# Seven block products in place of eight for four fifths of the q and k projection, on one core of a Trainium2

## The chip, the cores and the metric

The kernel runs on one core of one Trainium2 chip. The metric is the device time of the whole program in microseconds (us): the median of three runs before the change is 1844.57 us (1844.24 to 1844.73). The engines are named as in the profile: PE (matrix products), DVE (vector), ACT (scalar, activation), POOL (GpSimd) and SP, whose queue issues the transfers. SBUF is the memory on the chip, PSUM the eight banks into which PE writes.

## The reference

The computation takes x (2048 tokens of 640 numbers) through attention with 32 heads of 20 and through a Fourier mixing of tokens and columns, and blends the two by a gate.

```python
qkv = (x @ wqkv).reshape(B, S, 3, H, Dh).transpose(2, 0, 3, 1, 4)
q, k, v = qkv[0], qkv[1], qkv[2]
p = softmax(einsum("bhqd,bhkd->bhqk", q, k) * Dh ** -0.5)
a = (p @ v).transpose(0, 2, 1, 3).reshape(B, S, D) @ wo
ya, yb = x @ dft_hid_re.T, x @ dft_hid_im.T
b = dft_seq_re @ ya - dft_seq_im @ yb
g = sigmoid((x * gate_w).sum(-1, keepdims=True))
out = g * a + (1 - g) * b
```

The change touches the first line only, and of it the columns of q and k: 640 columns of weights each, that is five blocks of 128 (ND = 5), for four blocks of 512 tokens.

## The kernel before, in words

Every float32 value is split into two parts of a shorter type (float32r): a copy rounded to the short type, and the remainder, rounded as well. `split` (L112) does it with a copy on one engine (L114 on ACT, L116 elsewhere) and a subtraction on another (L117). A product of two such values is three matmuls, `three` (L119 to L122): high by high, high by low, low by high.

Tokens lie transposed in `xs[t]`, t = 0 to 3, each with its two parts, five blocks of 128 input columns (`d`) and 512 tokens. The q and k projection yields one tile per output block c (0 to 4 for q, 5 to 9 for k) and token block t: `qk_tiles` (L337) sums five terms of three matmuls, 15 matmuls of 512 columns, in one PSUM bank; ACT copies the bank into a tile `p` (L345), POOL splits that (L116, L117), and SP stores it to `qk_scr` in DRAM. From there SP loads, for each pair of heads, the twelve pieces of a "stack" into `kst` and `qst`, on which the score matmuls run (`s_mm`, L188). A score matmul (L198) fills a bank, and a maximum over it (L200, DVE) frees it.

PSUM banks for q, k, v and scores come from one ring, `bank()` (L129): a new tile takes the bank of the tile five places earlier, and the matmul waits until that one has been read. One of the six places is set aside for attention's output (`av`, L249). The two others hold the hidden-transform sums `yp`.

The work in order of program: block 0 of q and k for four token blocks, with the first v products between them (`v_pair`, L357: two tiles of 15 matmuls of 320 columns; POOL clears the tile, ACT copies); the rest of v; then the other eight column blocks, in the order 1, 6, 2, 7, 3, 8, 4, 9, each with four token blocks. At the head of each of these stands a `segment` (L402): eight score matmuls (ten in one of them) and one tile of the hidden transform (`hid_tile`, L374: 30 matmuls of 320 columns on half the rows each, whose two sums ACT copies at L395 and POOL adds at L396). Four times two more steps of scores are put in (`run_s`, L417; a step is two score matmuls). By the end of that stage 41 steps (LEAD) and 8 hidden tiles (HEAD) are done; the main loop follows, in which attention, the rest of the hidden transform and the token transform are interleaved. Each engine runs its instructions in the order in which the program lists them; SP issues all transfers in one row and waits in place where a tile isn't ready.

The tiles rotate in pools of a fixed number of buffers: `p` 7, `raw` 5 (raw weights, 1024 columns), `part` 2 (split weights), `v` 2. The four stack tiles kst and qst are not in use until the first stack is loaded.

## Time and profile before

| | |
|---|---|
| median of 3 runs | 1844.57 us (1844.24 to 1844.73) |
| profiled execution | 1844.95 us, of which the span is 1843.2 us |
| mean granted PE clock | 1.000 |
| PE matmuls | 17568 |
| DMA, mean | 282.12 MB, 153 GB/s |
| first q and k, v, other q and k, main loop, tail | 0 to 21, to 106, to 249.5, to 1838, to 1843.2 us |

The table's stage ends are read from the timeline. In the profile's rows an instruction has its engine, its line, the tiles (out<-in) and the shape; a matmul row's duration overlaps with the next, so the distance of two starts is what a matmul costs. "[idle before <-releaser]" at the end tells how long the engine stood before that row and what let it go on.

### The profile page before, as it was taken

How to read it: one execution, taken by the hardware profiler on the slowest of the kernel's cores; microseconds unless marked ns; L12 is line 12 of the kernel's file. 1: busy time of each engine (PE TensorE's matmuls, PEld its weight loads, DVE VectorE, ACT ScalarE, POOL GpSimd, SP SyncE). 2: the span in 40 equal slices, each digit the busy share in tenths (PEclk: the TensorE clock that was granted, in tenths of full speed). 3: DMA queues.
4: the chain of work that ended last, by engine and by line, in shares of the span. 5: the costliest groups of instructions: out<-in, count | busy, mean ns of one | idle time of the engine just before them, and what ended most of it. 6: DMA issues, size and time to landing. Idle time of an engine off the chain costs nothing.

```text
span 1843.2 us, 44645 instructions
## 1 busy us (share of the span) xinstructions
PE 1835.5 (100%) x17568; PEld 1359.3 (74%) x17568; DVE 1382.1 (75%) x2344; ACT 1354.7 (73%) x2646; POOL 1000.1 (54%) x819
## 2 busy tenths in 40 slices
PE   9999999999999999999999999999999999999998
PEld 8988777676767777777777777777777777776666
DVE  4044458888887888888888888888888888888843
ACT  4222258788787888888888888888888877778885
POOL 5234532121136676344677788655668867745644
PEclk9999999999999999999999999999999999999999
DMA  7654341222135574547577676746485866532233
GB/s 235 165 148 158 137 127 56 80 65 69 56 93 172 179 218 147 150 126 196 176 206 227 181 241 201 193 140 183 148 230 182 248 190 188 172 92 63 75 100 109
DMA packets 181898, 282.12 MB, mean 153 GB/s; under 512 B 47843, under 2 KB 116067, under 8 KB 181687
## 3 DMA queue, kind: packets, MB, share of 16 engines
q1 hardware_dynamic: 181687, 279.26, 50.8%
q8 instruction: 138, 2.26, 0.5%
q14 instruction: 73, 0.60, 0.1%
HBM read 215.14 MB, written 64.05 MB: 151 GB/s over the span
## 4 chain that ended last, share of the span: by engine, by line
PE 97%; POOL 1%; issue 1%; ACT 0%; DMA 0%; SPq 0%; DVE 0%; POOLq 0%; ACTq 0%; DVEq 0%
PE ps L566 25%; PE yp L645 20%; PE ps L959 17%; PE ps L198 14%; PE yp L385 7%; PE ps L120 3%; PE ps L122 3%; PE ps L121 3%; PE yp L752 3%; POOL p L117 1%; DMA raw<-in_xa 0%; ACT p L345 0%; POOL p L116 0%; POOL raw L396 0%; PE ps L1045 0%
## 5 line engine op out<-in xcount | busy, mean ns | idle before, releaser
L200 DVE TENSOR_REDUCE mx<-ps 128x1 f32<-128x512 f32 x2048 | 1279.1, 683 | 311.5 <-PE ps L198 250.9
L961 ACT ACTIVATE p<-ps 128x512 f32<-128x512 f32 x2048 | 1053.6, 613 | 277.8 <-PE ps L198 154.9
L959 PE MATMUL ps<-qst,kst 62*128 62x512 f32 x1920 | 726.2, 406 | 0.1
L198 PE MATMUL ps<-kst,qst 60*128 60x512 f32 x1920 | 665.7, 410 | 0.0
L645 PE MATMUL yp<-x,part 64*128 64x320 f32 x5376 | 628.7, 306 | 0.0
L645 PEld LDWEIGHTS yp<-x,part 64*128 64x128 f32 x5376 | 602.4, 185 | 5.6
L566 PE MATMUL ps<-p,v 128*21 128x512 f32 (+1 forms) x4096 | 479.2, 595 | 0.0
L117 POOL TENSOR_TENSOR part<-raw,part 128x1024 fp32r<-128x1024 f32 (+1 forms) x128 | 287.5, 2246 | 335.3 <-ACT part L114 305.5
L959 PEld LDWEIGHTS ps<-qst,kst 62*128 62x128 f32 x1920 | 341.3, 185 | 162.8 <-DVE mx L200 97.4
L198 PEld LDWEIGHTS ps<-kst,qst 60*128 60x128 f32 x1920 | 322.3, 184 | 12.7 <-issue 4.2
L566 PEld LDWEIGHTS ps<-p,v 128*21 128x21 f32 (+1 forms) x4096 | 104.0, 101 | 244.5 <-issue 237.3
L385 PE MATMUL yp<-wb,x 64*128 64x320 f32 x1920 | 224.1, 307 | 0.0
L385 PEld LDWEIGHTS yp<-wb,x 64*128 64x128 f32 x1920 | 210.1, 186 | 6.0
L396 POOL TENSOR_TENSOR raw<-raw 128x320 f32<-128x320 f32 x64 | 55.5, 868 | 264.6 <-ACT raw L395 219.9
L525 POOL TENSOR_TENSOR raw<-raw,raw 128x1024 f32<-128x1024 f32 x77 | 187.6, 2437 | 0.0
L114 ACT ACTIVATE part<-raw 128x1024 fp32r<-128x1024 f32 (+2 forms) x123 | 123.7, 1006 | 0.9 <-DMA raw<-in_wfirst 0.9
L752 PE MATMUL yp<-x,part 64*128 64x320 f32 x768 | 102.2, 308 | 0.0
L345 ACT ACTIVATE p<-ps 128x512 f32<-128x512 f32 x40 | 23.8, 597 | 106.4 <-PE ps L122 76.4
L117 POOL TENSOR_TENSOR x<-araw,x 128x320 fp32r<-128x320 f32 x112 | 97.6, 879 | 1.3
L752 PEld LDWEIGHTS yp<-x,part 64*128 64x128 f32 x768 | 91.9, 186 | 1.1
L120 PE MATMUL ps<-x,part 128*128 128x512 f32 x200 | 80.0, 400 | 0.5
L121 PE MATMUL ps<-x,part 128*128 128x512 f32 x200 | 78.5, 392 | 0.8 <-DVE x L117 0.8
(98 smaller groups left out, 1346.0 us busy)
## 6 DMA issues: line engine op xcount, KB each, us to landing
raw<-in_cdft SPq DMA_DIRECT2D x192, 512.0 KB
araw<-a_scr SPq DMA_DIRECT2D x192, 160.0 KB
qk_scr<-p SPq DMA_DIRECT2D x40, 512.0 KB
kst<-qk_scr SPq DMA_DIRECT2D x90, 160.0 KB
qst<-qk_scr SPq DMA_DIRECT2D x90, 160.0 KB
yt<-y_scr SPq DMA_DIRECT2D x80, 160.0 KB
a_scr<-raw SPq DMA_DIRECT2D x64, 160.0 KB
y_scr<-yt SPq DMA_DIRECT2D x64, 160.0 KB
```

Source lines behind the costliest of these rows:

```text
L117: e2.tensor_tensor(dst2, src, f32(dst1), op=ALU.subtract)
L120: pe.matmul(ps, st1, mv1, start=first, stop=False)
L121: pe.matmul(ps, st1, mv2, start=False, stop=False)
L198: pe.matmul(ps, q[b : b + KROWS, qt * P : (qt + 1) * P], k[b : b + KROWS, kc * 512 : (kc + 1) * 512], start=True, stop=True)
L200: return lambda: dve.tensor_reduce(mx[n][:, h, qt, kc : kc + 1], ps, axis=AX.X, op=ALU.max)
L385: pe.matmul(yp[h][:, :HE], x[r, xz, d, cs], w[r, wz, d, :HE], start=d == 0 and z == 0, stop=d == ND - 1 and z == 2)
L525: pool.tensor_tensor(raws[0], raws[0], raws[1], op=ALU.add if PRODUCTS[n][0][1][0] > 0 else ALU.subtract)
L566: pe.matmul(t[32 * j : 32 * j + m, :], v[:, r : r + m], pp[qc][:, h, :], start=kt == 0, stop=kt == NS - 1)
L645: pe.matmul(yp[h][:, :HE], c[r, cz, cs], a[r, az], start=s == 0 and z == 0, stop=s == NS - 1 and z == 2)
L752: pe.matmul(yp[h][:, :HE], o[oz][r], wos[d, hf][r, wz], start=d == 0 and z == 0, stop=end)
L959: pe.matmul(pt, k[b : b + KROWS + 2, kt * P : (kt + 1) * P], q[b : b + KROWS + 2, qc * 512 : (qc + 1) * 512], start=True, stop=True)
L961: act.activation(pts[n, kt, qc][:, h], pt, AF.Exp, scale=float(DH) ** -0.5)
```

## The change

Blocks 1 to 4 of q and of k are taken in pairs (c, 5 + c), and the tokens in two halves, g = 0 (token blocks 0 and 1) and g = 1 (2 and 3). The four results of a pair and a half (q and k, two token blocks) are one 2 by 2 block product whose inner dimension is also cut in two: input blocks 0, 1 against 2, 3. It is computed by Winograd's form with seven products in place of eight; the products of input block 4 are added into p5, p2 and p4 as they are, and into p3 on a difference of token blocks. `quad` has the seven in the order p6, p7, p1, p5, p2, p4, p3, with 6, 6, 6, 9, 9, 9 and 9 matmuls, and after them the sums of products: ACT copies three banks, DVE makes six additions with a PSUM operand (L444), POOL one (L459). Each of the four results is then split by ACT (copy, L112) and POOL (subtraction, L115) and stored as before.

The form needs sums of tokens and of weights. `load_sums` loads the tokens of a half again in float32, makes five sums on POOL (L384) and splits them on ACT and DVE; they live where the stacks will be (kst, qst, and x3 in the first half; kst1, qst1 and the place of x0 in the second). x0 is loaded once more in the main loop (`reload_x`, on POOL). `load_pair` loads a pair's weights, makes five sums on POOL (`sums`, L403 to L407), splits the summed ones (`ready`: ACT and DVE, 256, 384 and 384 columns) and the rest (`parts`: 640 and 384 columns, subtractions on DVE in the first half and on POOL in the second). While quad c runs, the pair c + 1 is made ready: sums after p5, `ready` after p2, `parts` after p4.

The program's order becomes: block 0 for token blocks 0 and 1; 8 v pairs with the first half's sums; four quads of the first half, without segments; block 0 for token block 2, two v pairs, for token block 3, six v pairs, the last three with two steps of scores each; four quads of the second half, each with one segment before p6 and one after p5, the first also with two steps of scores after p2. Hidden tiles take token blocks 4 to 15 of 128 first. `raw` has 4 buffers, `part` 3, and the bank ring has six places until the main loop.

```diff
-    for t in kst:
-        pool.memset(f32(t), 1.0)
...
-        return work.tile([P, 1024], F32, name="raw", bufs=5)
+        return work.tile([P, 1024], F32, name="raw", bufs=4)
 
     def part_tile():
-        return work.tile([P, 2, 1024], R, name="part", bufs=2)
+        return work.tile([P, 2, 1024], R, name="part", bufs=3)
...
+    def load_sums(g):
+        a = {}
+        for i, k in ((1, 0), (1, 1), (0, 0), (0, 1)):
+            a[i, k] = pair_tile()
+            sp.dma_start(a[i, k], xa[2 * g + i, :, 2 * k : 2 * k + 2])
+        b = pair_tile()
+        sp.dma_start(b, xa[2 * g : 2 * g + 2, :, ND - 1].rearrange("t p c -> p t c"))
+        if g:
+            more = new_x(0).rearrange("p z d c -> p (z d c)")
+            homes = [kst[1], qst[1], more[:, :S], more[:, S : 2 * S], more[:, 2 * S : 2 * S + 1024]]
+        else:
+            homes = [*kst, *qst, xs[3].rearrange("p z d c -> p (z d c)")[:, :1024]]
+        ops[g] = [t.rearrange("p (z d c) -> p z d c", z=2, c=512) for t in homes]
+        yield
+        s1, s2, s3, s4, s5 = ops[g]
+        sums = (
+            (s1, a[1, 1], a[1, 0], a[1, 1], ALU.add),
+            (s3, a[1, 0], a[0, 0], a[1, 0], ALU.subtract),
+            (s2, a[0, 0], a[1, 1], a[0, 0], ALU.subtract),
+            (s4, a[0, 1], a[0, 1], a[0, 0], ALU.subtract),
+            (s5, b[:, :1], b[:, :1], b[:, 1:], ALU.subtract),
+        )
+        for t, u, u1, u2, op in sums:
+            pool.tensor_tensor(u, u1, u2, op=op)
+            yield
+            split(t[:, 0], t[:, 1], u, act, dve)
+            yield
+
+    ops = {}
+    T_AT = ((0, 1), (3, 4), (5, 6), (2, 7))
+    B_AT = ((0, 1), (2, 3), (5, 6), (4,), (7,))
+
+    def load_pair(c, e2=dve):
+        a, b = raw_tile(), raw_tile()
+        n = ND * P
+        for k, raw in ((c, a), (ND + c, b)):
+            sp.dma_start(raw[:, :n].rearrange("p (d c) -> p d c", d=ND), wqk[k])
+        near, far, t13 = [slice(2 * P * k, 2 * P * (k + 1)) for k in range(2)] + [slice(n, n + 2 * P)]
+        made = {}
+
+        def sums():
+            t1, t3, t2 = a[:, t13], b[:, t13], b[:, near]
+            pool.tensor_tensor(t1, b[:, near], a[:, near], op=ALU.subtract)
+            pool.tensor_tensor(t3, b[:, far], b[:, near], op=ALU.subtract)
+            pool.tensor_tensor(t2, b[:, far], t1, op=ALU.subtract)
+            for k, raw in enumerate((a, b)):
+                pool.tensor_tensor(raw[:, 7 * P :], a[:, (2 + k) * P : (3 + k) * P], t2[:, k * P : (k + 1) * P], op=ALU.subtract)
+
+        def ready():
+            t = made["t"] = part_tile()
+            for o, u in ((3 * P, b[:, near]), (5 * P, b[:, n:]), (0, a[:, n:])):
+                w = slice(o, o + u.shape[1])
+                split(t[:, 0, w], t[:, 1, w], u, act, dve)
+
+        def parts():
+            t = made["b"] = part_tile()
+            split(t[:, 0, :n], t[:, 1, :n], a[:, :n], act, e2)
+            split(t[:, 0, n:], t[:, 1, n:], b[:, 2 * P : n], act, e2)
+
+        return made, sums, ready, parts
+
+    def quad(c, g, w, between):
+        x, y = xs[2 * g], xs[2 * g + 1]
+        s1, s2, s3, s4, s5 = ops[g]
+        made = w[0]
+
+        def group(*terms):
+            ps = bank()
+            todo = []
+            for name, k, z in terms:
+                at = (T_AT if name == "t" else B_AT)[k]
+                todo += [(made[name][:, :, o * P : (o + 1) * P], z[:, :, d]) for d, o in enumerate(at)]
+            for k, (wo_, z) in enumerate(todo):
+                three(ps, wo_[:, 0], wo_[:, 1], z[:, 0], z[:, 1], k == 0, k == len(todo) - 1)
+            return ps
+
+        def done(st, i, j):
+            split(st[:, 0].bitcast(R), st[:, 1].bitcast(R), st[:, 1], pool if g and c == ND - 1 else act, pool)
+            r = (j * ND + c) * P
+            stores.append((qk_scr[:, 2 * g + i, r : r + P].rearrange("z p c -> p z c"), st))
+            flush(2)
+
+        def add(out_, a, b):
+            dve.tensor_tensor(out_, a, b, op=ALU.add)
+
+        o12, o22 = pair_tile(), pair_tile()
+        p6 = group(("t", 1, s2))
+        act.activation(o12[:, 1], p6, AF.Copy)
+        between(0)
+        p7 = group(("t", 2, s3))
+        o11, o21 = pair_tile(), pair_tile()
+        p1 = group(("b", 0, x[:, :, 0:2]))
+        act.activation(o11[:, 0], p1, AF.Copy)
+        add(o12[:, 1], o12[:, 1], p1)
+        add(o21[:, 1], o12[:, 1], p7)
+        p5 = group(("t", 0, s1), ("b", 4, y[:, :, ND - 1 :]))
+        act.activation(o22[:, 0], p5, AF.Copy)
+        add(o12[:, 1], o12[:, 1], p5)
+        pool.tensor_tensor(o22[:, 1], o21[:, 1], o22[:, 0], op=ALU.add)
+        between(1)
+        done(o22, 1, 1)
+        p2 = group(("b", 1, x[:, :, 2:4]), ("b", 3, x[:, :, ND - 1 :]))
+        add(o11[:, 1], o11[:, 0], p2)
+        done(o11, 0, 0)
+        between(2)
+        p4 = group(("t", 3, y[:, :, 2:4]), ("b", 3, y[:, :, ND - 1 :]))
+        add(o21[:, 1], o21[:, 1], p4)
+        between(3)
+        done(o21, 1, 0)
+        p3 = group(("b", 2, s4), ("b", 4, s5))
+        add(o12[:, 1], o12[:, 1], p3)
+        done(o12, 0, 1)
...
     def hid_tile(i, read_out):
+        if j == 0:
+            st = (st + 4) % NS
...
+    def quads(g, soon, rest):
+        for c in range(1, ND):
+            this = soon[c - 1]
+            after = soon[c] if c + 1 < ND else None
+
+            def between(k):
+                if k == 0:
+                    if c + 2 < ND:
+                        soon.append(load_pair(c + 2, pool if g else dve))
+                    elif c + 2 == ND:
+                        soon.extend(rest[0]())
+                elif k == 1 and g:
+                    lead(0, 5, 8, 2)
+                if k and after:
+                    after[k]()
+                elif k in (1, 2):
+                    rest[k]()
+                if g and k == 2 and c == 1:
+                    run_s(step + 2)
+                if g and k == 2 and c == ND - 1:
+                    load_v(0)
+
+            if g:
+                lead(0, 5, 6, 4, 0) if c == ND - 1 else lead(0, 5, 8, 2)
+            quad(c, g, this, between)
+
+    fins = []
+    quads(0, soon, (lambda: fins.extend(load_wqk(k) for k in (0, ND)) or [], lambda: fins.pop(0)(), lambda: fins.pop(0)()))
+    fin = load_x(3)
+    pool.memset(f32(kst[0]), 1.0)
+    qk_tiles((0, ND), 2)
+    v_pair(0, 8)
+    fin()
+    sums = load_sums(1)
+    next(sums)
+    v_pair(0, 10)
+    qk_tiles((0, ND), 3)
+    flush()
+    stack = list(load_stack(0))
+    for s in (12, 14):
+        v_pair(0, s)
+        flush()
+        for args in stack[3 * s - 36 : 3 * s - 30]:
+            sp.dma_start(*args)
+        next(sums)
+        if s == 14:
+            next(sums)
+    soon = [load_pair(1, pool)]
+    for s in range(8, NS, 2):
+        v_pair(1, s)
+        if s == 8:
+            flush()
+            fin = load_wb(2)
+        else:
+            run_s(step + 2)
+        if s < 14:
+            next(sums), next(sums)
+        if s == 10:
+            fin()
+        if s == 12:
+            soon[0][1]()
+            soon[0][2]()
+            soon.append(load_pair(2, pool))
+        if s == 14:
+            next(sums)
+            soon[0][3]()
+    make_gate()
+    quads(1, soon, (lambda: fins.append(load_wb(3, act, pool)) or [], lambda: fins.pop()(), lambda: None))
+    pool.memset(f32(kst[1]), 1.0)
+    xs[0] = new_x(0)
+    av["name"] = places.popleft()
+    av["tile"] = place_tile(av["name"])
...
+    for k, d in enumerate(range(0, ND, 2)):
+        prepare(1 + 4 * k, 4 + 4 * k, reload_x, d)
```

In the second half DVE stands for c = 1, from p2's addition to the start of the next segment, as follows (ps0 to ps5 are banks; L444 frees the bank that it reads, L198 in this numbering is the maximum over scores, L115 the remainder of `split`):

```order
L444 TENSOR_TENSOR p_1648<-p_1648,ps5_1742 128x512
L115 TENSOR_TENSOR part_1756<-raw_1502,part_1756 128x256
L115 TENSOR_TENSOR part_1756<-raw_1502,part_1756 128x384
L115 TENSOR_TENSOR part_1756<-raw_1501,part_1756 128x384
L198 TENSOR_REDUCE mx_1414<-ps0_1763 128x1
L198 TENSOR_REDUCE mx_1414<-ps1_1765 128x1
L198 TENSOR_REDUCE mx_1414<-ps2_1769 128x1
L198 TENSOR_REDUCE mx_1414<-ps3_1771 128x1
L444 TENSOR_TENSOR p_1649<-p_1649,ps4_1775 128x512
L444 TENSOR_TENSOR p_1627<-p_1627,ps5_1794 128x512
L198 TENSOR_REDUCE mx_1414<-ps0_1808 128x1
L198 TENSOR_REDUCE mx_1414<-ps1_1810 128x1
```

In the stage of before, DVE has these rows from the end of one segment to the head of the next (L200 is the maximum there, L117 the remainder):

```order
L200 TENSOR_REDUCE mx_1024<-ps3_1238 128x1
L200 TENSOR_REDUCE mx_1024<-ps4_1240 128x1
L117 TENSOR_TENSOR part_1274<-raw_1111,part_1274 128x640
L200 TENSOR_REDUCE mx_1024<-ps4_1342 128x1
L200 TENSOR_REDUCE mx_1024<-ps0_1344 128x1
L200 TENSOR_REDUCE mx_1024<-ps1_1348 128x1
```

Between two segments stood one weight subtraction that wanted no sum; now three that do stand there, ahead of the four maxima of the lone scores and of two additions that free banks.

POOL has, for the same quad of the second half, the hidden transform's sum (L522), the five sums of weights, then two remainders of results (o22, o11) and the weights' remainders:

```order
L459 TENSOR_TENSOR p_1628<-p_1649,p_1628 128x512
L522 TENSOR_TENSOR v_1729<-v_1729 128x320
L403 TENSOR_TENSOR raw_1501<-raw_1502,raw_1501 128x256
L404 TENSOR_TENSOR raw_1502<-raw_1502 128x256
L405 TENSOR_TENSOR raw_1502<-raw_1502,raw_1501 128x256
L407 TENSOR_TENSOR raw_1501<-raw_1501,raw_1502 128x128
L407 TENSOR_TENSOR raw_1502<-raw_1501,raw_1502 128x128
L115 TENSOR_TENSOR p_1628<-p_1628 128x512
L115 TENSOR_TENSOR p_1648<-p_1648 128x512
L115 TENSOR_TENSOR part_1786<-raw_1501,part_1786 128x640
L115 TENSOR_TENSOR part_1786<-raw_1502,part_1786 128x384
```

Before, one hidden sum (L396) stood between the casts and remainders of single results:

```order
L396 TENSOR_TENSOR raw_1248<-raw_1248 128x320
L116 CAST p_1268<-p_1268 128x512
L117 TENSOR_TENSOR p_1268<-p_1268 128x512
L116 CAST p_1295<-p_1295 128x512
L117 TENSOR_TENSOR p_1295<-p_1295 128x512
```

The sums of weights that DVE's subtractions need now stand behind the hidden sum on POOL.

In the first half DVE has, around the next pair's weights (c = 2; the rows up to the next quad's first addition):

```order
L444 TENSOR_TENSOR p_764<-p_764,ps2_797 128x512
L115 TENSOR_TENSOR part_811<-raw_648,part_811 128x256
L115 TENSOR_TENSOR part_811<-raw_648,part_811 128x384
L115 TENSOR_TENSOR part_811<-raw_647,part_811 128x384
L444 TENSOR_TENSOR p_765<-p_765,ps3_818 128x512
L115 TENSOR_TENSOR part_829<-raw_647,part_829 128x640
L115 TENSOR_TENSOR part_829<-raw_648,part_829 128x384
L444 TENSOR_TENSOR p_743<-p_743,ps4_837 128x512
L444 TENSOR_TENSOR p_851<-p_851,ps1_874 128x512
```

The 640-column subtraction, which the next quad's p1 needs (its third matmul takes the lower part), stands behind the `ready` subtractions and p4's addition. Before, the weights of a block were split one block ahead, in the one row shown above.

102 lines of the change are left out of this document (46 added, 56 removed).

## The prediction

> **What bounds the kernel now.** I read the busy times first, then the windows cut at the stage ends, then the list of TensorE's waits, and last the timeline of the stage that the change rewrites. The page gives TensorE (PE) the whole span:
>
> ```profile
> span 1843.2 us, 44645 instructions
> PE 1835.5 (100%) x17568; PEld 1359.3 (74%) x17568; DVE 1382.1 (75%) x2344; ACT 1354.7 (73%) x2646; POOL 1000.1 (54%) x819
> ```
>
> The windows (us; busy time of each engine, granted clock, DMA share, GB/s) say the same of the first stages, which end at 249.5 us, and that their other engines have room:
>
> ```profile
> 0.00:21.00 21.00, 18.75 (x79) 15.23 (x80) 11.86 (x15) 11.76 (x19) 9.71 (x12) 1.00 0.83 277
> 106.00:249.50 143.50, 143.12 (x802) 115.48 (x800) 59.01 (x97) 30.43 (x58) 69.77 (x70) 1.00 0.39 138
> 249.50:1838.00 1588.50, 1588.34 (x16149) 1146.29 (x16148) 1294.97 (x2218) 1285.75 (x2506) 894.58 (x708) 1.00 0.51 151
> ```
>
> PE's own waits are nothing after the start (line, what was waited for, us, times, longest):
>
> ```profile
> PE ps L425 <- POOL ident masks.py:199: 1.4, 1, 1.4
> PE ps L121 <- DVE x L117: 0.8, 2, 0.5
> ```
>
> So the time is PE's instructions, one behind the other. Whatever takes matmuls out saves their issue time, as long as nobody makes PE wait; the change puts most of its new work on DVE and POOL, so the question is whether PE then waits for them. The span is 1843.2 us; the profiled execution took 1844.95, with 1.75 outside the span, and stands 0.38 above the median of 1844.57.
>
> **PE: fewer matmuls.** One column block's matmuls follow each other like this (start, duration; 14 steps between the two rows):
>
> ```profile
> 112.73 0.39 PE L120 MATMUL ps<-x,part 128*128 128x512 f32 x1
> ...
> 115.94 0.40 PE L122 MATMUL ps<-x,part 128*128 128x512 f32 x1
> ```
>
> 3.21/14 = 0.229 us each. A pair of columns on two token blocks took 4 tiles of 15 = 60 matmuls. Its seven products take 6+6+6+9+9+9+9 = 54. Eight such quads: 48 fewer, 48 x 0.229 = **-11.0 us**. Scores, hidden-transform and v matmuls stay in number.
>
> **The price list.** DVE and POOL (operation, shape, count | busy, mean ns):
>
> ```profile
> L665 DVE TENSOR_TENSOR m<-yp,m 128x320 f32<-128x320 f32 x56 | 26.8, 479 | 0.0
> L117 DVE TENSOR_TENSOR part<-raw,part 128x640 fp32r<-128x640 f32 x8 | 6.6, 825 | 30.7 <-ACT part L114 30.7
> L117 DVE TENSOR_TENSOR part<-raw,part 128x256 fp32r<-128x256 f32 x5 | 2.1, 419 | 3.3 <-ACT part L114 3.3
> L117 POOL TENSOR_TENSOR part<-raw,part 128x512 fp32r<-128x512 f32 x16 | 20.6, 1289 | 1.3
> L117 POOL TENSOR_TENSOR p<-o,p 128x256 fp32r<-128x256 f32 x2 | 1.5, 730 | 0.7 <-ACT p L114 0.7
> L345 ACT ACTIVATE p<-ps 128x512 f32<-128x512 f32 x40 | 23.8, 597 | 106.4 <-PE ps L122 76.4 <-issue 18.6 <-POOL p L117 11.0
> L114 ACT ACTIVATE part<-raw 128x256 fp32r<-128x256 f32 x5 | 2.0, 405 | 0.9 <-DMA raw<-in_wfirst 0.9
> ```
>
> Worked out from these by width: DVE subtraction of 384 columns 0.56, 512 about 0.69, DVE add of 512 with a PSUM operand 0.68 (the 320 row plus 192 x 0.00106); POOL 128 columns 0.43, 384 about 1.0, 640 about 1.6; ACT 384 about 0.52. A pair's five weight sums on POOL (L403 to L407) are 3 x 0.73 + 2 x 0.43 = 3.05.
>
> DVE and POOL do not run freely beside each other. In the first three rows a 966-wide DVE subtraction starts under a POOL one; in the last two the POOL one starts under DVE's:
>
> ```profile
> 113.59 0.61 POOL L116 CAST p<-p 128x512 fp32r<-128x512 f32 x1 [2.65 <-ACT p L345]
> 114.28 1.29 POOL L117 TENSOR_TENSOR p<-p 128x512 fp32r<-128x512 f32 x1
> 114.46 2.88 DVE L117 TENSOR_TENSOR wb<-raw,wb 128x966 fp32r<-128x966 f32 x2 [3.27 <-ACT wb L114]
> 132.54 0.82 DVE L117 TENSOR_TENSOR part<-raw,part 128x640 fp32r<-128x640 f32 x1 [3.04 <-ACT part L114]
> 132.64 1.88 POOL L117 TENSOR_TENSOR p<-p 128x512 fp32r<-128x512 f32 x1
> ```
>
> POOL's 1.88 is 1.29 plus nearly all that was left of DVE's 0.82 (0.72); 0.13 overlapped. DVE's two (by width 1.17 and 0.83) took 2.88, 0.88 more, of 1.11 that POOL had left. So each holds the other off. [...] My sum lets each wait for the other's end, and leaves out the gap between two POOL operations (114.20 to 114.28, 0.08 us), which about cancels the overlap of 0.13.
>
> **Second half (quads with segments).** The present segment and its reductions:
>
> ```profile
> 124.10 0.74 PE L198 MATMUL ps<-kst,qst 60*128 60x512 f32 x4
> 124.63 4.87 DVE L200 TENSOR_REDUCE mx<-ps 128x1 f32<-128x512 f32 x8 [4.33 <-PE ps L198]
> 125.40 0.47 PE L198 MATMUL ps<-kst,qst 60*128 60x512 f32 x2
> 126.82 0.48 PE L198 MATMUL ps<-kst,qst 60*128 60x512 f32 x2
> 127.52 0.51 PE L120 MATMUL ps<-x,part 128*128 128x512 f32 x1
> 128.38 0.88 POOL L396 TENSOR_TENSOR raw<-raw 128x320 f32<-128x320 f32 x1 [1.54 <-ACT raw L395]
> ```
>
> From its first score: the last two scores at +2.72, the next matmul at +3.42, the reductions (0.61 each) done at +5.40, POOL's add at +4.28 to 5.16. I set a clock to zero at the first score of a quad's second segment (after p5). p2 ends at 3.42+2.06 = 5.48. POOL: hidden add to 5.16, the five sums behind it to 8.2, DVE's 256-wide weight subtraction let in (0.42) before the last: 8.63. Then o22's subtraction to 9.92, DVE's first 384 to 10.48, o11's to 11.77, DVE's second 384 to **12.33**. Without POOL's 2 x 1.29 in between it would be 9.85. Behind these on DVE stand the additions that free the banks of p4 and p3, and the reductions.
>
> Four lone scores, and the three gate operations that I need further down (first and last):
>
> ```profile
> 116.26 0.73 PE L198 MATMUL ps<-kst,qst 60*128 60x512 f32 x4
> 117.02 0.50 PE L120 MATMUL ps<-x,part 128*128 128x512 f32 x1
> 119.65 0.16 DVE L465 TENSOR_SCALAR gate<-gate 128x16 f32<-128x16 f32 x1
> 120.13 0.17 DVE L467 TENSOR_SCALAR ngate<-gate 128x16 f32<-128x16 f32 x1
> ```
>
> - c=1: four lone scores (117.02 - 115.94 - 0.23 = 0.85; their reductions stand behind 12.33 and are done at 12.94 to 14.77), p4 and p3 end PE's work at 10.45. The next segment's first four scores want those banks from 10.55; adds end 15.45, 16.13; scores 7 and 8 wait for its first two reductions, 16.74 and 17.35, against 13.4 wanted: 4.0 late.
> - c=2: the next segment starts at 9.7; adds 13.01 and 13.69, reductions 14.30 and 14.91, the eighth score wanted at 12.5: 2.4 late.
> - c=3: the next segment has ten scores; the tenth waits for the fourth reduction, 16.13, wanted at about 12.95: 3.2; the ten-score segment of before already holds 0.55 of that (below), so 2.65.
>
> ```profile
> 212.95 0.73 PE L198 MATMUL ps<-kst,qst 60*128 60x512 f32 x4
> 216.62 0.50 PE L198 MATMUL ps<-kst,qst 60*128 60x512 f32 x1
> 217.22 0.50 PE L120 MATMUL ps<-x,part 128*128 128x512 f32 x1
> ```
>
> (4.27 from first score to next matmul; 3.42 plus one extra pair at about 0.3 is 3.72, hence 0.55.) Together **+9.05**.
>
> **First half.** Clock at p6. p5 ends at 27 x 0.229 = 6.18, ACT's copy at 6.8, o22's add on POOL 8.14, sums with the 256-wide subtraction let in 11.61, o22's subtraction 12.90, DVE 384 13.46, o11's 14.75, DVE 384 15.31, add of p4 15.99, the 640 parts 16.82. The next quad's p1 wants these parts at 12.37 + 14 x 0.229 = 15.58: 1.24 late, three times: **+3.7**.
>
> **Joint.** The last v pair is followed by four lone scores and at once by a segment: twelve scores on six banks. From the first: four reductions to 2.97, then s5's subtraction (0.69, or up to 1.6 later behind POOL's 640 parts), three gate operations (0.65), then the segment's first two reductions at 4.9/5.5, or 7.1, which its last scores want at 3.6: 1.8 to 3.4, taken 2.6.
>
> **First scores on the first stack.** Its twelve loads now stand behind the second half's tokens on SP. From the shapes, 13.9 MB move between the start of the last quad of the first half and the first score, during (54 + 60) x 0.229 + 180 x 0.146 = 52.4 us of PE work (0.146 is 20.00/137 in the next row): 265 GB/s. The first window above moved 277 at a share of 0.83; this one, with v's short rows,
>
> ```profile
> 80.00:100.00 20.00, 20.00 (x137) 20.00 (x136) 1.91 (x2) 6.03 (x20) 2.76 (x5) 1.00 0.88 213
> ```
>
> would give 242 at full share, 57.4 us: late by 0 to 5.0. v is 2.1 MB of the 13.9, so it is nearer to the first: 0.4.
>
> **Edits at nothing.** Eight v pairs of 30 matmuls at 0.146 us are 35 us of PE. Under them lie the first half's sums of x on POOL (five, 11 us by the row below) and their splits; the second half's have the same cover. Six additions with PSUM per quad (4.1 us of DVE) are short beside 12.4 us of PE; ACT's splits go where POOL's casts went. One raw buffer fewer, and x's first block loaded again in the main loop (POOL, three pieces of up to 1.04 + 2.38 us in a loop where POOL is busy 895 of 1588.5 us): 0, at most 2 if a transform load is held up. Nothing here can gain beyond the matmuls, since PE had no wait to lose.
>
> ```profile
> L117 POOL TENSOR_TENSOR part<-raw,part 128x1024 fp32r<-128x1024 f32 x112 | 266.9, 2383 | 334.0 <-ACT part L114 305.5 <-DMA y_scr<-m 11.6 <-DMA raw<-in_cdft 9.4
> L116 POOL CAST part<-raw 128x1024 fp32r<-128x1024 f32 x2 | 2.1, 1038 | 0.1
> ```
>
> **Sum.** -11.0 + 9.05 + 3.7 + 2.6 + 0.4 = +4.75: the profiled execution 1849.7, on the median's footing **1849.3**.
>
> **Rivals.**
> - *DVE and POOL do not delay each other so* (operations slip past, or ACT's copies come late enough that they interleave at no cost). The weight subtractions end at 9.85: c=1 1.5 late, c=2 nothing, c=3 0.15, first half nothing, joint 1.8, stack 0.4: 3.85 of stalls, **1837.4**. It decides the sign: the break-even of 11.0 us of stalls lies between. If the rest hides too, 1833.6. [...] Against it: the two pairs of rows above.
> - *The stack is late*: DMA at the rate of the v window, 4.6 more: **1853.9**, up to 1860 with waits in the loads of the pairs behind it. Against it: the first window's rate.
> - *POOL doesn't yield*: its parts (1.6 and 1.0) go ahead of DVE's subtractions, which end at 14.9 instead of 12.33, in three quads: +7.7, **1857**. No row shows POOL back to back with DVE waiting.
> - That the change does not do what it says can't be here: 48 matmuls are gone from PE's list.
>
> **Chances.** A measurement of this kernel tells 0.2% (3.7 us) from no change: faster is below 1840.9, slower above 1848.3. My forecast 0.46 (1845 to 1853: 0.34 slower, 0.12 same), free interleaving 0.38 (0.34 faster, 0.04 same), late stack 0.10, POOL first 0.06 (both slower). The range leaves out the lowest quarter of the second (0.09) and most of the last two (0.10): 1836 to 1855.5. The forecast's own range is 1845 to 1853.
>
> **What would show it.** PE's waits for bank releases by DVE (L198's reductions, L444's additions) of 2 to 4 us at the first segment of c=2, 3 and 4, and for DVE's parts at p1 in the first half; DVE's 256 and 384 subtractions longer than 0.42 and 0.56, with POOL's p subtractions beside them. The prediction is wrong if PE's busy time in the first stages doesn't fall by about 11 us, if those waits sum to under 11, or if the main loop's length moves by over 2.

## The result, and the profile after

The kernel became slower: 1866.97 us (median of 4 runs, 1865.15 to 1868.31) against 1844.65 (median of 4) for the kernel before, a ratio of 1.0121 with a 95% interval of 1.0103 to 1.0138. That is clear of the 0.2% that count as no change, and outside the range of the forecast. The profiled execution took 1868.31 us.

The page and the clock line of the profile after (the 40 slices are 46.7 us each; the fourth, 140 to 187 us, lost clock):

```profile
span 1866.5 us, 44873 instructions
PE 1841.1 (99%) x17520; PEld 1359.7 (73%) x17520; DVE 1448.6 (78%) x2426; ACT 1392.5 (75%) x2716; POOL 1057.8 (57%) x859
PEclk9998999999999999999999999999999999999999
```

The 48 matmuls are gone, yet PE is now idle for 25 us. The largest groups of its waits (what it waited for: us, times, longest), where before there were three short waits of 2.2 us in all:

```profile
PE ps L196 <- DMA qst<-qk_scr: 5.8, 2, 3.1
PE ps L196 <- DVE p L444: 3.7, 2, 2.6
PE ps L196 <- DVE mx L198: 2.9, 2, 1.7
PE ps L120 <- DVE part L115: 2.3, 4, 0.9
PE ps L118 <- ACT part L112: 2.2, 1, 2.2
```

The windows by stage (us, busy times, granted clock, DMA share, GB/s) show where, and that the main loop, from 271.6 us on, hardly changed: what was 249.5 us of lead is 271.6, 22.1 of the 23.3 us of the span.

```profile
56.00:120.00 64.00, 59.53 (x248) 47.01 (x248) 37.76 (x51) 30.56 (x62) 39.81 (x37) 0.97 0.56 183
...
153.70:160.50 6.80, 1.02 (x3) 0.28 (x1) 0.69 (x1) 1.83 (x5) 2.87 (x2) 0.73 1.05 257
160.50:167.00 6.50, 6.46 (x23) 5.87 (x24) 4.57 (x6) 2.14 (x4) 3.54 (x3) 0.50 0.55 152
167.00:271.60 104.60, 97.08 (x576) 76.82 (x574) 78.86 (x123) 34.20 (x71) 57.41 (x57) 0.95 0.33 111
271.60:1861.00 1589.40, 1588.36 (x16145) 1146.25 (x16146) 1295.76 (x2218) 1285.27 (x2504) 909.33 (x720) 1.00 0.52 152
```

Two things stand there that the profile before did not show at all. From 153.7 to 160.5 us PE does almost nothing while the DMA is full; and from 160.5 to 167 it is busy all the time at half the clock. PE's two waits there, for the last loads of the stack, after a v matmul that started at 153.66:

```profile
157.05 0.76 PE L196 MATMUL ps<-kst,qst 60*128 60x512 f32 x1 [3.09 <-DMA qst<-qk_scr]
160.54 0.89 PE L196 MATMUL ps<-kst,qst 60*128 60x512 f32 x2 [2.73 <-DMA qst<-qk_scr]
```

The same slow pace follows another wait, at the second quad of the first half (start, duration; a matmul's cost is the distance to the next start); the last three rows are from the quad after it, where a shorter wait leaves the pace as it was:

```profile
68.89 0.40 PE L120 MATMUL ps<-x,part 128*128 128x512 f32 x1
71.46 0.80 PE L118 MATMUL ps<-kst,part 128*128 128x512 f32 x1 [2.17 <-ACT part L112]
72.06 0.63 PE L119 MATMUL ps<-kst,part 128*128 128x512 f32 x1
72.48 0.63 PE L120 MATMUL ps<-kst,part 128*128 128x512 f32 x1
...
74.98 0.39 PE L120 MATMUL ps<-qst,part 128*128 128x512 f32 x1
75.21 0.39 PE L118 MATMUL ps<-qst,part 128*128 128x512 f32 x1
...
90.47 0.50 PE L120 MATMUL ps<-x,part 128*128 128x512 f32 x1 [0.95 <-DVE part L115]
90.81 0.40 PE L118 MATMUL ps<-x,part 128*128 128x512 f32 x1
91.04 0.39 PE L119 MATMUL ps<-x,part 128*128 128x512 f32 x1
```

After 2.2 us without work the matmuls cost 0.43 us instead of 0.229 for 3.2 us. The trace's clock record agrees: 0.50 from 71.47 us for 3.41 us. Taking from every step between two matmul starts its steady cost (0.229, 0.148, 0.116 and 0.074 us for the four shapes), I get what PE lost place by place; before the change such losses summed to 6.5 us from 21 to 249.4 us, after it to 39.6 from 21 to 271.5 us, 33.1 more, and 33.1 - 11.0 for the matmuls is the 22.1. About half of the 33.1 shows as idle time (2.6 us of the lead before, 19.4 after); the rest shows as busy time, most of it from matmuls at half pace: PE's busy time in the lead rose from 246.9 to 252.2 us although 48 matmuls are gone. By place, each to about 0.2 us:

| place | forecast, us | lost, us |
|---|---|---|
| first half, p1's parts, three times | 3.7 | 3.2 |
| first half, second quad's p6 with the slow pace behind (4.0), and 0.5 ahead of it | 0 | 4.5 |
| first scores on the stack with the slow pace behind | 0.4 | 9.7 |
| joint of lone scores and segment (5.06, less the 0.7 that an undisturbed segment loses here) | 2.6 | 4.4 |
| second half, the three next segments (5.35, 2.43, 5.27, less 0.7 each) | 9.05 | 10.9 |
| main loop (23.3 - 22.1) | 0 | 1.2 |

The row of DVE in the second half came out nearly as worked out. The second segment of its first quad starts at 189.24 us (first row), and the ready subtractions end at 201.25, 12.01 us later where I had 12.33:

```profile
189.24 0.74 PE L196 MATMUL ps<-kst,qst 60*128 60x512 f32 x4
```

```profile
197.28 0.43 DVE L115 TENSOR_TENSOR part<-raw,part 128x256 fp32r<-128x256 f32 x1 [1.24 <-ACT part L112]
198.62 2.63 DVE L115 TENSOR_TENSOR part<-raw,part 128x384 fp32r<-128x384 f32 x2 [0.91 <-ACT part L112]
201.17 2.47 DVE L198 TENSOR_REDUCE mx<-ps 128x1 f32<-128x512 f32 x4
203.56 1.27 DVE L444 TENSOR_TENSOR p<-p,ps 128x512 f32<-128x512 f32 x2
```

### The profile page after: what moved, and what is told of

Read it like the earlier page. It is cut to its first block, busy times and chain, and to the rows that moved or that the text cites. A ratio compares the mean times of both kernels' runs of the same rounds, so it can differ in the third digit from the quotient of the medians.

```text
span 1866.5 us, 44873 instructions
## 1 busy us (share of the span) xinstructions
PE 1841.1 (99%) x17520; PEld 1359.7 (73%) x17520; DVE 1448.6 (78%) x2426; ACT 1392.5 (75%) x2716; POOL 1057.8 (57%) x859
## 4 chain that ended last, share of the span: by engine, by line
PE 90%; DMA 2%; issue 2%; POOL 2%; DVE 2%; ACT 1%; SPq 0%; POOLq 0%; DVEq 0%; ACTq 0%
PE ps L749 25%; PE yp L828 19%; PE ps L1144 17%; PE ps L196 14%; PE yp L511 7%; PE yp L935 3%; PE ps L118 2%; PE ps L120 2%; PE ps L119 2%; DVE part L115 1%; DVE mx L198 1%; DMA v_scr<-v 0%; DMA qst<-qk_scr 0%; DMA raw<-in_xa 0%; DVE p L444 0%
## 5 line engine op out<-in xcount | busy, mean ns | idle before, releaser
L198 DVE TENSOR_REDUCE mx<-ps 128x1 f32<-128x512 f32 x2048 | 1279.4, 683 | 255.8 <-PE ps L196 183.8
L1146 ACT ACTIVATE p<-ps 128x512 f32<-128x512 f32 x2048 | 1053.7, 613 | 282.4 <-PE ps L196 151.1
L196 PE MATMUL ps<-kst,qst 60*128 60x512 f32 x1920 | 674.6, 412 | 13.9 <-DMA qst<-qk_scr 5.8
L115 POOL TENSOR_TENSOR part<-raw,part 128x1024 fp32r<-128x1024 f32 (+3 forms) x136 | 299.4, 2203 | 339.9 <-ACT part L112 329.1
L196 PEld LDWEIGHTS ps<-kst,qst 60*128 60x128 f32 x1920 | 326.4, 185 | 30.4 <-DVE mx L198 7.1
L511 PE MATMUL yp<-wb,x 64*128 64x320 f32 x1920 | 229.9, 310 | 0.4 <-ACT raw L521 0.4
L522 POOL TENSOR_TENSOR raw<-raw 128x320 f32<-128x320 f32 x56 | 48.6, 867 | 228.0 <-ACT raw L521 190.9
L112 ACT ACTIVATE part<-raw 128x1024 fp32r<-128x1024 f32 (+3 forms) x157 | 138.5, 898 | 8.3 <-POOL raw L407 4.0
L115 POOL TENSOR_TENSOR x<-araw,x 128x320 fp32r<-128x320 f32 x112 | 97.5, 877 | 1.3
L731 POOL TENSOR_TENSOR araw<-araw 128x320 f32<-128x320 f32 x80 | 70.1, 887 | 0.2 <-DMA araw<-a_scr 0.2
L115 POOL TENSOR_TENSOR p<-p 128x512 fp32r<-128x512 f32 x40 | 54.6, 1379 | 25.6 <-ACT p L112 25.1
L962 POOL TENSOR_TENSOR yt<-yt,m 128x320 f32<-128x320 f32 x64 | 55.9, 886 | 2.3 <-DVE m L848 2.3
```

Source lines behind the costliest of these rows:

```text
L112: act.activation(dst1, src, AF.Copy)
L115: e2.tensor_tensor(dst2, src, f32(dst1), op=ALU.subtract)
L196: pe.matmul(ps, q[b : b + KROWS, qt * P : (qt + 1) * P], k[b : b + KROWS, kc * 512 : (kc + 1) * 512], start=True, stop=True)
L198: return lambda: dve.tensor_reduce(mx[n][:, h, qt, kc : kc + 1], ps, axis=AX.X, op=ALU.max)
L511: pe.matmul(yp[h][:, :HE], x[r, xz, d, cs], w[r, wz, d, :HE], start=d == 0 and z == 0, stop=d == ND - 1 and z == 2)
L731: pool.tensor_tensor(raws[0], raws[0], raws[1], op=ALU.add if PRODUCTS[n][1][1][0] > 0 else ALU.subtract)
```

## The experiments

All times are medians; each ratio is to the kernel before, run beside it, with its 95% interval.

| run | edit | us | before, us | ratio (interval) |
|---|---|---|---|---|
| 1 | matmuls in the stack's wait | 1863.88 | 1844.88 | 1.0107 (1.0092 to 1.0122) |
| 2 | stack's loads first | 1868.59 | 1844.88 | 1.0128 (1.0113 to 1.0143) |
| 3 | x2's split later | 1864.50 | 1844.88 | 1.0108 (1.0091 to 1.0125) |
| 4 | ready behind p3 | 1868.36 | 1844.88 | 1.0125 (1.0110 to 1.0140) |
| 5 | ready on POOL | 1853.13 | 1844.18 | 1.0049 (1.0034 to 1.0064) |
| 6 | lone scores in the quads | 1866.97 | 1844.18 | 1.0126 (1.0109 to 1.0143) |
| 7 | 3, 5 and 6 | 1853.00 | 1844.18 | 1.0049 (1.0034 to 1.0064) |
| 8 | 7, and p1's parts first | 1852.82 | 1844.18 | 1.0047 (1.0032 to 1.0062) |
| 9 | 8, x not read again | 1852.78 | 1844.52 | 1.0043 (1.0028 to 1.0058) |
| 10 | 8, sums and ready earlier | 1851.83 | 1844.52 | 1.0038 (1.0023 to 1.0053) |
| 11 | 10, 2 MB loaded earlier | 1844.67 | 1844.52 | 1.0002 (0.9992 to 1.0011) |
| 12 | 11, stack's rest later | 1844.60 | 1844.62 | 0.9996 (0.9987 to 1.0005) |
| 13 | 12, last v tile cleared earlier | 1848.38 | 1844.61 | 1.0023 (1.0014 to 1.0032) |
| 14 | 13, o11's split later | 1844.95 | 1844.61 | 1.0004 (0.9995 to 1.0013) |
| 15 | 12, o11's split later | 1840.93 | 1844.78 | 0.9979 (0.9970 to 0.9988) |
| 16 | 15, v stores first | 1840.18 | 1844.78 | 0.9974 (0.9964 to 0.9984) |
| 17 | 16, last v tile cleared earlier | 1841.55 | 1844.58 | 0.9980 (0.9971 to 0.9989) |

**1. Matmuls in the wait.**

```diff
+            if s == 10:
+                y = new_y(0)
+                for _ in range(29):
+                    pe.matmul(y, xs[1][:, 0, 0, :P], xs[1][:, 0, 0], start=True, stop=True)
             run_s(step + 2)
```

> The changed kernel with 29 matmuls of 512 columns whose product nobody reads, put before the first lone scores, where TensorE stood for 6.6 us (153.7 to 160.5 us of its profile) and its matmuls then ran at about half pace for 6 us. Theory A (the gap takes the clock down; a TensorE that has something to do keeps it): the wait stays, the half pace behind it goes, 3 us faster than the changed kernel, about 1864. Rival B (the slow pace comes from the busy DMA or from memory, not from the gap): no faster, 1867 or up to 1 us more.

3.3 us less than the changed kernel, as theory A had it; the intervals overlap, but the trace decides. PE's rows around the 29 matmuls, and the windows:

```profile
151.91 6.79 PE L655 MATMUL yp<-x 128*128 128x512 f32 x29
158.62 0.84 PE L196 MATMUL ps<-kst,qst 60*128 60x512 f32 x4
159.65 0.32 PE L119 MATMUL ps<-wb,x 128*128 128x322 f32 x1
159.80 0.31 PE L120 MATMUL ps<-wb,x 128*128 128x322 f32 x1
```

```profile
149.00:157.00 8.00, 8.00 (x44) 7.09 (x43) 1.23 (x1) 1.95 (x6) 3.03 (x2) 1.00 1.01 197
157.00:164.00 7.00, 7.00 (x42) 6.05 (x40) 3.77 (x6) 1.20 (x2) 1.97 (x3) 1.00 0.89 240
```

The DMA is as busy as before, the clock stays at 1.00 and v's matmuls cost 0.15 us each from the second one on, where they cost 0.27 behind the gap (two starts there are 162.10 and 162.37 us). The gap makes the slow pace, not the DMA.

**2. The stack's loads first.**

```diff
-    stack = list(load_stack(0))
+    for args in load_stack(0):
+        sp.dma_start(*args)
     for s in (12, 14):
         v_pair(0, s)
         flush()
-        for args in stack[3 * s - 36 : 3 * s - 30]:
-            sp.dma_start(*args)
```

> The changed kernel with all twelve loads of the first stack issued right after the stores that they read, ahead of the v stores of four pairs. Theory A (the loads come late because SP issues them behind v stores that wait for their tiles): the wait of 6.6 us falls to 2 or less and the half pace behind it goes: 6 to 9 us faster than the changed kernel, 1858 to 1861. Rival B (the transfers are bound by their rate; whatever goes first, the last byte comes at the same time, and the v tiles now wait): 0 to 2 us faster.

No gain: rival B. The wait changed its name. What PE waited for is now partly the copies of v (L491), which wait for POOL to clear v tiles, which waits for v's stores:

```profile
PE ps L196 <- ACT logit L491: 3.2, 1, 3.2
PE ps L196 <- DMA qst<-qk_scr: 2.2, 2, 1.7
```

```profile
158.72 0.66 POOL L483 MEMSET v<- 128x672 f32 x1 [13.78 <-DMA v_scr<-v]
```

**3. x2's split later.** In the first quad after p5, instead of ahead of it (`fin()` moved into `between(1)`).

> The changed kernel with the split of the third token block (3 ACT copies, 3 DVE subtractions) moved from before the first quad into it, after p5. Theory A (these hold ACT and DVE 5.5 us at the head of the first quad, so the weights of the second come 2.3 us late and the clock falls): the wait at the second quad's p6 and the half pace behind it go, 3 to 4 us faster. Rival B (ACT is late anyway, because the copies of the last v pair wait for a v tile to be stored): 0 to 1.5 us faster.

2.5 us less, between the two, and with overlapping intervals; p6's wait is 1.4 us in its profile. In the profile of run 4, whose first half is the changed kernel's, it is 1.0, so this wait varies by itself and the run settles little.

**4. Ready behind p3.**

```diff
         add(o12[:, 1], o12[:, 1], p3)
+        between(4)
         done(o12, 0, 1)
+        between(5)
```

(`ready` is called at 4 and `parts` at 5 in the second half.)

> The changed kernel with the next pair's weight splits of the second half (ready, then parts) put behind p3's addition, so that the additions which free banks, and the four lone maxima, no longer stand behind them on DVE. Theory A (DVE's order makes the waits of 4.0, 1.6 and 4.0 us at the next segments): these fall to about 0.5 each, 7 to 9 us faster. [...]

No gain. The additions free their banks early now, but the next segment's maxima wait for the same subtractions, and these still take 4.35 us beside POOL's remainders (DVE's row, then POOL's, then PE's wait):

```profile
198.12 4.35 DVE L115 TENSOR_TENSOR part<-raw,part 128x256 fp32r<-128x256 f32 x3
```

```profile
195.00 5.26 POOL L115 TENSOR_TENSOR p<-p 128x512 fp32r<-128x512 f32 x4
200.22 3.11 POOL L115 TENSOR_TENSOR part<-raw,part 128x640 fp32r<-128x640 f32 x2
```

```profile
PE ps L196 <- DVE mx L198: 8.7, 4, 2.8
```

By their widths the three take 0.42 + 2 x 0.56 = 1.54 us. So moving them down DVE's row does not help; whether it is that they are on DVE beside POOL, the next run asks.

**5. Ready on POOL.**

```diff
-                split(t[:, 0, w], t[:, 1, w], u, act, dve)
+                split(t[:, 0, w], t[:, 1, w], u, act, e2)
...
-                if k and after:
+                if after and g:
+                    for n in {1: (1, 2), 3: (3,)}.get(k, ()):
+                        after[n]()
+                elif k and after:
                     after[k]()
```

> The changed kernel with the subtractions of the next pair's ready weights in the second half on POOL in place of DVE, right behind the five sums and ahead of the results' remainders. Moving them behind p3's addition on DVE gained nothing: there they took 4.35 us between POOL's remainders, where their own durations sum to 1.54. [...] Rival B (POOL, with 2.7 us more per quad, now ends the parts or the ready weights late, and p6 or p1 wait in turn): 0 to 3 us faster.

13.4 us less (22.3 above before, now 8.9): the three places went, with the slow pace behind them (512-column matmuls that do not wait follow each other in 0.34 us or less from 167 to 260 us, where half pace is 0.43). The edit changes two things, the engine and the place: on POOL the three stand right behind the sums, ahead of the results' remainders. DVE's subtractions in that early place were not run, so what the engine alone is worth is not shown. No wait of PE for L444 is left, and one for a maximum, at the joint:

```profile
PE ps L196 <- DMA qst<-qk_scr: 6.8, 2, 3.7
...
PE ps L196 <- DVE mx L198: 1.9, 1, 1.9
```

**6. Lone scores in the quads.** The three pairs behind v pairs go behind p2 of the quads c = 2, 3 and 4, the gate behind the first segment.

> The changed kernel with its three pairs of lone scores behind v pairs moved into the quads of the second half, behind p2 of each, and the gate behind the first segment: the first score is asked for some 13 us of TensorE work later, and the burst of twelve scores is gone. Theory A (the stack is bound by the rate of the transfers and comes at about 160 us whatever is done): its wait of 6.6 us with the slow clock behind (3.2) and the burst (4.7) go, 14.6 us; the lone maxima of two quads now stand behind the ready weights as those of the first do, 2 to 5 us back: 9 to 12 us faster, 1855 to 1858. Rival B (the loads only start later, because their stores and v's move too, or the first segment waits in place of the lone scores): 0 to 5 us faster.

No gain: rival B. The first segment now waits, for v's copies, and the lone maxima stand behind the ready weights in every quad:

```profile
PE ps L196 <- DVE mx L198: 6.5, 3, 3.2
PE ps L196 <- ACT logit L491: 6.1, 2, 3.3
```

**7 and 8. The edits together, and p1's parts first.** Run 7 is 3, 5 and 6. Run 8 adds, in the first half, the 640-column subtraction in pieces of 256 and 384, ahead of p4's addition.

> Three edits together: the third token block's split inside the first quad, the ready subtractions of the second half on POOL, the lone scores in the quads. Theory A (the waits are apart from each other): 2.5 + 8 + 14.6 us faster than the changed kernel, with nothing back, since DVE has no subtraction ahead of the lone maxima: about 1842, level with the kernel before or up to 4 us faster. Rival B (one cover was shared; POOL or ACT ends late): 1848 to 1856.

> The same three edits, and in the first half the 640-column parts subtraction in two pieces (256 columns, which the next p1 needs, and 384), put ahead of p4's addition. Theory A (p1 waits for DVE's row as worked out: 1.12 us at two quads, less at one): 2 to 3 us faster than with three edits. [...]

Run 7 is no faster than run 5 alone, and run 8 no faster than run 7, though p1's waits for DVE fell from 3.0 to 1.3 us. What was won ahead of the first segment was waited for there: 10.2 us in run 7, 9.5 in run 8, for the copies of v. (Run 8's line:)

```profile
PE ps L196 <- ACT logit L495: 9.5, 2, 6.2
```

**9. x not read again.** The second half's sums are made from the high parts of x in SBUF; the low parts are left out of them.

> The kernel of the last run (four edits) with the second half's sums of x made from the high parts of x that lie in SBUF, so that 2.6 MB are not read again between the first half's quads and the first score; the low parts are left out of these sums, so they are less precise. In the last run TensorE waits 9.5 us at the first segment for ACT's copies of v, which wait for v tiles, which wait for v's stores, with the DMA busy at 0.8 to 1.0. Theory A (bytes: that stretch is bound by the rate of the transfers, about 245 GB/s, and 2.6 MB are 10.6 us): the wait and the slow clock behind it go, 8 to 11 us faster than with the four edits, 1842 to 1845. Rival B (latency: a v tile's store takes as long whatever else is loaded): 0 to 4 us faster.

Theory A fell. The DMA share from 130 to 140 us is 0.32 where run 8 has 0.89, but the wait is 8.8 us and the time the same. First run 9's windows, then run 8's:

```profile
130.00:140.00 10.00, 10.00 (x61) 9.35 (x60) 0.00 (x0) 3.24 (x6) 5.57 (x5) 1.00 0.32 115
150.00:160.00 10.00, 10.00 (x69) 10.00 (x68) 1.49 (x1) 1.84 (x5) 3.04 (x2) 1.00 1.02 259
```

```profile
130.00:140.00 10.00, 10.00 (x59) 9.18 (x58) 0.00 (x0) 3.23 (x6) 4.63 (x4) 1.00 0.89 260
```

The bytes of the whole stretch do not decide. The last ten microseconds are full in both (1.02 in run 8 as well). The rows of SP, POOL and ACT in run 9 show what stands behind what: a v store stands on SP behind the stack's pieces, POOL's clearing of the next v tile waits for an earlier one, and ACT waits for the hidden transform's weights, asked for behind all of them:

```profile
143.54 5.43 SPq L663 DMA_DIRECT2D qst<-qk_scr  x6
152.03 0.38 SPq L346 DMA_DIRECT2D v_scr<-v  x1
153.09 2.26 SPq L331 DMA_DIRECT2D raw<-in_wb  x2
```

```profile
160.12 0.66 POOL L499 MEMSET v<- 128x672 f32 x1 [6.19 <-DMA v_scr<-v]
```

```profile
161.08 1.64 ACT L112 ACTIVATE wb<-raw 128x966 fp32r<-128x966 f32 x2 [7.66 <-DMA raw<-in_wb]
```

**10. Sums and ready earlier in the first half.** `sums` at `between(0)` and `ready` at `between(1)`.

> The four edits, and in the first half the next pair's weight sums at the head of the quad and its ready weights after p5, each a step earlier. TensorE waits there 2.7 us at the second quad's p6 and 1.3 at p1. Theory A (whatever is won ahead of the stretch that is bound by the transfers is waited for at its end: the quads' end only asks earlier): the waits in the first half fall by 2 us or more and the wait at the first segment grows by as much, the time stays within 1 us of 1852.8. Rival B (the wins add): 2 to 4 us faster.

1852.8 became 1851.8: theory A. p6's wait is gone, and the wait at the first segment is 9.2 us.

**11. 2 MB loaded earlier.**

```diff
+    for args in load_half(0, 0):
+        sp.dma_start(*args)
     v_pair(0, 8)
...
+                if k == 2 and not g and c == ND - 1:
+                    load_ahead()
```

(`load_half(0, 0)` is the first stack for token blocks 0 and 1; `load_ahead` loads two of the five tiles for the second half's sums into `raw` tiles.)

> All these, with 2 MB moved out of the bound stretch to where the DMA is at 0.6: the first stack's pieces for token blocks 0 and 1 are loaded right after the first of the other two blocks' q and k products, and two of the five tiles for the second half's sums while the last quad of the first half runs. Theory A (bytes): 5 to 9 us faster than the four edits, 1844 to 1848. Rival B (the stretch is not bound by bytes, or the earlier loads only push v's stores): within 2 us of 1852.8.

7 to 8 us less than runs 8 and 10; level with the kernel before. The two moves were not tried apart; since taking 2.6 MB of x away gained nothing in run 9, the stack's half is the likelier, which is argued and not shown.

**12 to 17. The rows of SP and POOL, and o11.** Run 12 puts the hidden transform's weights first and the stack's second half behind the first two of the last four v pairs. Run 13 clears the last v tile ahead of the pair's sums on POOL. Run 14 also makes the first half's parts ahead of o11's split; run 15 does that without run 13's edit. Run 16 issues each v store ahead of the stack's pieces; run 17 is 16 with 13's edit.

> The last kernel with SP's row changed: the second half of the first stack is loaded behind the first two v pairs of the last four (six pieces behind each) instead of ahead of and between the two before them, and the hidden transform's weights are asked for before the pair's. Taking 2.6 MB away left the wait at the first segment as it was (8.8 against 9.5 us), so the bytes of the whole stretch are not its cause. Theory A (a v store behind six to twelve loads of the stack takes 7 to 8 us to land, and with two v tiles POOL's clearing, ACT's copies and SP's next store wait for it in turn; stack and weights are wanted only at 158 us): v's stores land sooner, the wait of 5.7 us at the first segment falls to 3 or less with the slow clock behind it, 3 to 6 us faster, 1839 to 1842. Rival B (the stack's loads land late instead, and the first score waits for them): within 2 us of 1844.7.

> The last kernel with the first pair's weight sums and ready weights of the second half emitted behind the last v pair instead of ahead of it, so that POOL clears the last v tile 8 us earlier (it did so at 162 us, behind the sums, though its tile was free) and ACT empties the bank for which the first segment waits. Theory A (POOL's row): the wait of 3.0 us at the first segment and what follows it go, 2 to 4 us faster than the last kernel, 1841 to 1843. Rival B (the tile comes free late, from the transfers, or p6 now waits for the weights): within 1 us.

> The same, and in the first half o11's split behind the next pair's parts, so that ACT makes these about 0.6 us earlier. Theory A (nothing behind takes it up any more): p1's three waits of 0.6 us and the slowed steps with them (0.77 each) go, 1.5 to 2.5 us faster than the run before. Rival B (the v stage's end still depends on transfers that start no earlier): 0 to 0.5 us.

> The kernel of the twelfth run (loads reordered) with o11's split of the first half behind the next pair's parts, and POOL's row as it was there. In the last pair of runs this edit was worth 3.4 us. Theory A (the first half's gain is kept as far as the wait at the first segment does not take it up): 1 to 3.5 us faster than 1844.6, so 1841 to 1843.5. Rival B (it is taken up, the wait grows by as much): 1844 to 1845.

> The same with each v store of the last four pairs issued as soon as its pair is done, ahead of the stack's pieces that follow it. Theory A (a v store behind the stack's pieces lands late and holds up the v tile for the last pair): the wait of 3 us at the first segment and the slow clock behind it go, 3 to 5 us faster than the run beside it, 1837 to 1840. Rival B (SP now stands until ACT has copied the pair, and the stack's last pieces land after the first score wants them): within 1 us, or slower.

> The last kernel (v stores first) with POOL's clearing of the last v tile ahead of the first pair's weight sums, as in the thirteenth run, where it gained nothing because the store that it waits for stood behind the stack's pieces. Theory A (both were needed: the store early and the clearing early): the clearing comes at about 155 us, the wait of 2.3 us at the first segment and the slow pace behind it go, 2 to 4 us faster than 1840.2. Rival B (the store takes 7 us or more to land in any case, or the weights, which now come behind it, are late for p6): the same time or 1 to 4 us slower, as in the thirteenth run.

Run 12's time did not move, though its wait for v's copies fell from 5.7 to 3.0 us: neither theory as written. Run 13 was slower: the clearing waited for the store that SP had behind the stack's pieces, and the pair's weights came behind it.

```profile
161.56 0.66 POOL L502 MEMSET v<- 128x672 f32 x1 [9.59 <-DMA v_scr<-v]
```

Run 14 against 13 and run 15 against 12 show that the first half's gain is kept now, 3.4 and 3.7 us, more than p1's waits (1.8 us in runs 12 and 13). Run 16 and run 15 cannot be told apart, and neither can 17: its clearing comes at 155.0 us as expected, but PE then waits 4.0 us for a maximum and 2.3 us for a hidden sum:

```profile
PE ps L201 <- DVE mx L203: 4.0, 1, 4.0
PE yp L532 <- ACT raw L542: 2.3, 1, 2.3
```

Runs 15 to 17 are faster than both kernels, by 0.20 to 0.26% against the one before. What the last 2 to 3 us at the first segment need stays open; a third buffer for v, the direct test of its loop of stores and clearings, was not run.

## Why the prediction was wrong

The direction held, the sum did not: 22.3 us slower where it said 4.75. Two of its own three signs of being wrong came in: PE's busy time in the first stages rose by 5.3 us instead of falling by about 11, and the named waits for DVE sum to 8.9 us in the list above, under 11, though counted by lost steps, slow pace included, the same places come to 18.5. The main loop moved by 0.9, under 2. By its own steps:

- **PE's 48 matmuls, -11.0.** Right: 17520 instead of 17568, and the losses of 33.1 less 11.0 give the 22.1 of the lead.
- **Second half, +9.05.** The mechanism was right (DVE's weight subtractions are held up beside POOL's, 2.63 us for two that take 1.12 by width, and the next segment waits), 10.9 measured with the slow pace that I had not priced. Two of the three places have a stretch at half clock behind them, worth 1.6 and 1.9 us; without these it is 7.4 us, so that the total came near 9.05 is partly luck. Run 5 takes the three subtractions off DVE and the waits go; run 4 shows that a later place on DVE is not enough. The lower rival, that DVE and POOL do not delay each other, is refuted by the 2.63 us that two subtractions of 0.56 took. (Its 9.85 should be 9.75, 12.33 less 2 x 1.29; that moves the rival by a few tenths at most.)
- **First half, +3.7.** 3.2 measured, 1.1 at the later two quads where I had 1.24. At the first, p1 waited only 0.3 us in this trace, after p6 had already been held up; in the traces of runs 1, 2, 4, 5 and 6, whose first half is the same, that wait too is 1.2 us.
- **Joint, +2.6.** 4.4, of which the slow clock behind it is 2.0 (0.59 from 180 to 184 us). Without it 2.4, near the forecast.
- **First scores on the stack, 0.4: the first step that failed.** "v is 2.1 MB of the 13.9, so it is nearer to the first." I had both ends, 0 and 5.0 us, and took the lower because few of the bytes were v's. It lost 9.7. The wait itself, 6.6 us from 153.66 to 160.54 less two steps, is a little over the upper end of 5.0; the other 3 us are the slow clock behind it (run 1). The slower of my two rates was the measured one: 241 GB/s from 99.1 to 160.5 us, at a DMA share of 0.80, so the transfers were not at full share throughout. And rate against bytes does not settle it: moving all loads first (run 2) or taking 2.6 MB away (run 9) changed nothing in the time. What the rows show instead is that v's stores, v's two tiles and the stack's pieces wait for each other in one row. That sum was of bytes over time, where SP's order and the two buffers of v had to be followed, transfer by transfer. Which link of that row sets the end stays open: runs 11, 12 and 16 shorten the wait and none removes it.
- **Edits at nothing: failed in part.** The v products were to hide the first half's sums, but the last v pairs drain late themselves. ACT's rows in the profile after: PE was done with the last v pair at 56.3 us, ACT copied it at 60.7, since POOL's clearing at 60.00 had waited 4.7 us for a store, and split x2 behind it:

```profile
60.69 0.45 ACT L487 ACTIVATE v<-ps 128x320 f32<-128x320 f32 x1 [1.92 <-POOL v L483]
61.44 2.55 ACT L112 ACTIVATE x<-p 128x1024 fp32r<-128x1024 f32 x3
```

So the second quad's weights came 2.2 us late: 4.0 us with the slow pace. This size belongs to this one execution: in the traces of runs 1, 2, 4, 5 and 6 the wait is 0.5 to 1.0 us and no slow pace follows. The first half as a whole loses 6.0 to 7.6 us there, against 7.7 here, so a loss of 2 us and more over the forecast stands in all of them.

- **What I had left out altogether: the clock, the second step that failed.** Each wait of 2 us and more in the first stages (2.17, 3.09 with 2.73, and 2.56 us) was followed by half-pace matmuls. The five stretches at half clock in this trace cost about 1.7, 3.3, 2.0, 1.6 and 1.9 us beyond the steady cost of their matmuls, 10.5 together; with the 6.2 by which the stack's wait alone passed its 0.4, that is 16.7 of the 17.6 us that the forecast missed. The profile before had no such wait, and its clock was 1.00 to the end of the main loop, so no row there gave this price. Behind the wait of 2.2 us the rows above show 3.2 us of half pace, the clock record 3.41. A shorter one, of 1.2 us at 178.75 us in the same trace, was followed by the half clock too. A wait of 1.9 us in run 5, at 178.41 us, was not, so in that range the length alone does not decide.

The three named rivals: the late stack came nearest (1853.9, up to 1860) and names the largest loss, though without the slow clock behind it; POOL first did not happen (0.43 us of DVE, at 197.28 us above, were let in between two POOL operations); free interleaving did not.

## What to carry to other kernels

A wait on an engine that never waited can cost more than its length: where the clock dropped behind it, waits of PE of 1.2 to 2.6 us cost 1.6 to 2.0 us more here, 3.4 us at half pace. Where a stage runs with two buffers and one row of transfers, follow the buffers' stores through that row before calling anything hidden, and don't credit a win ahead of a stage that is bound by transfers until that stage is mended (runs 7, 8 and 10 gave nothing, the same kind of edit in 14 and 15 gave 3.5 us). And where two engines hold each other off, as DVE and POOL did here, operations are dear when both have them queued back to back (4.35 us for 1.54 in run 4): putting DVE's three on POOL, at an earlier place, was worth 13 us.
